# Keeping half instead of a quarter of one streamed weight chunk in SBUF, with a kept chunk's rest and the transposes moved in PSUM

## The chip, the cores and the metric

The kernel runs on one core of one Trainium2 chip. The metric is the device time of one execution in microseconds (us). Besides the matrix engine TensorE (PE, with its weight loads shown apart as PEld) the core has VectorE (DVE), ScalarE (ACT), GpSimd (POOL) and SyncE (SP). DMAs are issued from the queues of SP, ACT and POOL.

## The reference

Two independent results stand side by side in the output. Half A multiplies a shifted and weighted `k` by `v`, convolves it along 2048 positions with a long filter by way of FFTs, adds a skip term, and multiplies by `q`. Half B is a recurrent attention over 64 segments of 32 rows. Its loop is what matters here:

```python
mem = mem0                                        # 8 rows of 1024
for s in range(n_seg):                            # 64 segments
    h = concatenate([mem, x[:, 32*s:32*s+32]])    # 40 rows
    q = einsum('btd,dhe->bhte', h, Wq)            # 32 heads of 128; k and v alike
    p = softmax(where(mask, einsum('bhqe,bhke->bhqk', q, k) * scale, -1e9))
    o = einsum('bhqk,bhke->bhqe', p, v)
    o = einsum('bhte,hed->btd', o, Wo)
    mem = o[:, :8]                                # feeds the next segment
    outs.append(o[:, 8:])
```

The first eight rows of a segment's output are the memory of the next, so the segments run one after another. Wq, Wk, Wv and Wo are 1024 x 4096 (or 4096 x 1024) in bf16, 32 MB together, more than SBUF holds.

## The kernel before, in words

**Two stages.** The first 440 us or so compute half A (`a_kernel`), and beside it, by `fill` and `dense`, the queries, keys and values of the rows that every segment brings itself; these go to the DRAM tensors `REC` and `VBD`. `x_block` turns the rows of x, and stores them in `REC` with one DMA of GpSimd per four segments. In this stage a scheduler decides the order of instructions. The second stage is the loop over 64 segments; I call one turn of it a pass. Its order is written out by hand, under `tc.manual_schedule()`: each engine runs its instructions in the order of the code, and waits at each for what it needs.

**Weights.** A weight chunk is 128 x 2048 bf16, 512 KB. There are 64: eight each of (Wk, Wq, Wv) x two halves g, and sixteen of Wo. 48 live in SBUF for the whole loop (tiles `Wres`, `Wmid`, `Wmore`, `Wlate`, `pw`, `Wring`). The other 16 are streamed (`STREAM`). Two of those (`KEPT_A`, `KEPT_B`) are tucked away bit by bit in unused PSUM columns in pass 0 (`keep`), and in every later pass VectorE copies them back, a quarter at a time (`quarter`, `quarter_b`; in place of `wring`). So 14 come from the DRAM copy `WS` in every pass, through a ring of five slots `wring` (`fetch`, issued from SP in order: the next chunk goes out when PE has finished with the slot's old one). Of one of them, `PART`, which is the chunk of Wo for head pair 4, the first quarter of the columns stays in the SBUF tile `part`, and a pass streams the other 384 KB.

**A pass, in PE's order.** `Proj(m, g)` accumulates a projection in a PSUM bank: four 32-column matmuls for each of eight chunks, about 0.22 us for a chunk. K uses bank `acc0`, Q `acc1`, V the bank g. `evac` is ScalarE's copy of the result to SBUF (`qkv_sb`). Then `transposes` turns it on PE into PSUM, and VectorE (K and Q of g = 0) or ScalarE (g = 1) copies it out to `KT` or `QT`. The hand-written order puts other chunks between an evacuation and its transposes, to cover it. `scores`, `softmax_a`, `softmax_b`, `attend` follow for each g; `out_half` multiplies by Wo into `yacc` (the same two banks). `fill_mem` turns the eight memory rows of the result, through the PSUM tile `tps`, into the next pass's `hT` (`rec`).

**PSUM.** Each partition has eight banks of 2 KB: the banks `acc0` and `acc1`, one bank `tps` (two rows of 512 bf16), one bank `SB` for scores, four for `OTp`. Chunk `KEPT_B` has four quarters, spread over unused columns (`B_homes`); the last quarter is partly in SBUF (`B_rest`, 768 bytes), and PE reads that part straight from there. Before, the transposes of K0, Q0 and K1 go to `tps[:, 0, :]`, and those of Q1 to bank 1, whose name is then `turned`:

```python
q0.run(4)
KT0 = keys(0)
nc.vector.tensor_copy(KT0[:, :, :, 0:32], transposes(k0, True))
q0 = q0.run(2).evac()
...
nc.scalar.copy(KT1[:, :, :, 0:32], transposes(k1))
turned = transposes(q1, tp=bank(1, "turned")[:].bitcast(BF)[:, 0:512])
```

**Descriptors.** `set_scratch` cuts the room in which GpSimd's DMAs keep their descriptors to `SCRATCH` bytes in each partition.

Of the kernel before, what the change touches and what calls it, by code (L numbers as in the profile page):

```python
# [9 lines left out]
BF = mybir.dt.bfloat16  # L10
F32 = mybir.dt.float32
I32 = mybir.dt.int32
# [8 lines left out]

FIRST, LAST = (0, 1, 2, 3), (10, 15, 11, 12, 14)
KEPT_A, KEPT_B = (3, 13, 0), (3, 9, 0)
PART = (3, 4, 0)
O_ORDER = (*FIRST, 4, 5, 6, 7, 9, 13, 8, *LAST)
ORDER = [(0, kc, 0) for kc in (0, 1, 4, 5)] + [(1, kc, 0) for kc in (0, 1)] + [(0, kc, 0) for kc in (2, 3, 6, 7)] + \
    [(1, kc, 0) for kc in range(2, 8)] + [(m, kc, 1) for m in (0, 1) for kc in range(8)] + \
# [8 lines left out]
RING = 5  # L36

PITCH = 2048
SCRATCH = 1024


def set_scratch(nc, size):
    cut = nc.dynamic_dma_scratch_size - size
    nc.lookup_mloc("DynamicDMAScratchLoc").dims = [128, size]
    nc.lookup_mls("DynamicDMAScratchLoc").tensor_shape = [128, size]
    nc.dynamic_dma_scratch_size = size
    for name in ("const-float32-0.0", "const-float32-1.0", "const-bfloat16-1.0", "const-uint8-127"):
        loc = nc.lookup_mloc(name)
        loc.addr = loc.addr - cut
    nc.sbuf_base = nc.sbuf_base - cut  # L50
# [372 lines left out]
def b_kernel(ctx: ExitStack, tc, x, mem0, Wq, Wk, Wv, Wo, outb, n_seg, run_a):  # L423
    nc = tc.nc
# [27 lines left out]
    def dram_chunk(ch):  # L452
        m, a, g = ch
        return Wo_v[a] if m == 3 else W_v[m][a, g]

    def dst_view(ap, ch):
        return ap.rearrange("p (hh d) -> p hh d", hh=2) if ch[0] == 3 else ap

    def stream_src(ch):
        return WS[ring_order.index(ch), :, 0:2048]  # L460
# [3 lines left out]
    REC = dram.tile([128, n_seg, 768], BF, name="REC")  # L464
# [33 lines left out]
    def pw(k=None):  # L498
        if k is None:
            k = pw_next[0] % 8  # L500
            pw_next[0] += 1
        return pring.tile([128, 2048], BF, tag=f"pw{k}", name="pw")
# [89 lines left out]
    def x_block(b):  # L592
        X_sb = loaded.pop(b)
        if b % 2 == 0:
            t = base.tile([128, 2048], BF, tag="wring3", name="xt")
            xts[b], xts[b + 1] = t[:, 0:1024], t[:, 1024:2048]
        tp = ps0.tile([128, 1024], BF, tag="ps0", name="xt_ps")
        for kc in range(8):
            nc.tensor.transpose(tp[:, kc * 128:(kc + 1) * 128], X_sb[:, kc * 128:(kc + 1) * 128], ident[:])
        xt = xts.pop(b).rearrange("p (s k t) -> p s k t", s=4, k=8)  # L600
        rows = tp[:].rearrange("p (k j t) -> p j k t", k=8, j=4)
        nc.vector.tensor_copy(xt[:, :, :, NM:SEG], rows[:, :, :, 0:NX])
        nc.vector.tensor_copy(xt[:, :, :, 0:NM], rows[:, :, :, NX:SEG])
        rec_stores.append(nc.gpsimd.dma_start(REC[:, 4 * b:4 * b + 4, 0:256], xt.rearrange("p s k t -> p s (k t)")))

    xts = {}
    rec_stores, x_loads = [], []
# [39 lines left out]
    q1 = [None] * 8  # L647
# [46 lines left out]
    def more(i):  # L694
        return wres3.tile([128, 2048], BF, tag=f"Wmore{i}", name="Wmore")
# [10 lines left out]
    live = {}  # L706
    now = [0]
    free = [4, 5, 0, 1, 3]

    def slot():  # L710
        k = free.pop(0)
        t = (base if k < 4 else ring).tile([128, 2048], BF, tag=f"wring{k}", name="wring")
        return k, t

    def fetch():
        if loads:
            s, ch = loads.pop(0)
            live[s, ch] = k, t = slot()
            if ch in kept:
                nc.sync.dma_start(dst_view(t[:], ch), dram_chunk(ch))  # L720
            elif ch == PART:
                nc.sync.dma_start(t[:, 512:2048], stream_src(ch)[:, 512:2048])
            else:
                nc.sync.dma_start(t[:], stream_src(ch))

# [13 lines left out]
    with c0p:  # L739
# [5 lines left out]
        for i, ch in enumerate(v_temp):  # L745
            if i >= 2:
                home = (lambda i=i: more(i)) if i < len(v_temp) - 2 else (lambda k=i - len(v_temp) + 4: pw(k))
# [3 lines left out]
        with tc.issue_after(got[-1].ins):  # L751
            for _ in range(2):
                fetch()
        n_k = len(own[0, 0])
        late = late[n_k:-2] + late[4:n_k] + late[:4] + late[-2:]
        for g in range(2):
# [13 lines left out]
            if g == 0:  # L770
# [8 lines left out]
    one = ctx.enter_context(tc.tile_pool(name="b_one", bufs=1, side="right", reuse_waits="tile"))  # L779
# [7 lines left out]
    tps = ps_t.tile([128, 2, 512], BF, name="tps")  # L787
    SB = ps_s.tile([128, 512], F32, name="SB")
    S = SB[:, 0:320].rearrange("p (b k) -> p b k", b=8)
    OTi, tpi, SBi = OTp[:].bitcast(I32), tps[:].bitcast(I32), SB[:].bitcast(I32)  # L790
    B_rest = one.tile([128, 192], I32, name="B_rest")
    B_homes = [[(tpi[:, 1, :], 0)], [(SBi[:, 320:448], 0), (OTi[:, :, 480:512], 128)], [(OTi[:, :, 416:480], 0)],
               [(B_rest[:], 0), (SBi[:, 448:512], 192)]]

    def bits(dst, src):
        nc.vector.tensor_scalar(out=dst, in0=src, scalar1=0, scalar2=None, op0=ALU.bitwise_or)  # L796

    def like(ap, home):
        return ap.rearrange("p (b x) -> p b x", b=4) if len(home.shape) == 3 else ap

    def quarter_b(q, tag):
        t = one.tile([128, 256], I32, tag=tag, name="quarter_b")
        w = []
        for home, at in B_homes[q]:
            n = home.shape[1] * (home.shape[2] if len(home.shape) == 3 else 1)
            if home.shape == B_rest[:].shape:
                part = home.bitcast(BF)
            else:
                bits(like(t[:, at:at + n], home), home)
                part = t[:].bitcast(BF)[:, 2 * at:2 * at + 2 * n]  # L810
            for dh, o in enumerate(quarter_cols(q)):
                lo, hi = max(at, 128 * dh), min(at + n, 128 * dh + 128)
                if lo < hi:
                    w.append((o + 2 * lo - 256 * dh, o + 2 * hi - 256 * dh, part[:, 2 * (lo - at):2 * (hi - at)]))
        return w

    def quarter_cols(q):
        return [1024 * (q // 2) + 512 * dh + 256 * (q % 2) for dh in range(2)]
# [27 lines left out]
    def pieces(ch):  # L846
        if ch in res:
            return [(0, 2048, res[ch])]
        if now[0] == 0 and ch in at_hand:
            return [(0, 2048, at_hand[ch][0])]  # L850
        if ch == PART:
            return [(0, 512, part[:]), (512, 2048, live[now[0], ch][1][:, 512:2048])]
        return [(0, 2048, live[now[0], ch][1][:])]

    def columns(ps, a, b):
# [13 lines left out]
                place_late(1, lambda: base.tile([128, 2048], BF, tag="wring2", name="Wring"))  # L869
            fetch()  # L870

    part = one.tile([128, 512], BF, name="part")
    nc.sync.dma_start(part[:], dram_chunk(PART)[:, 0, 0:512])
    P_pad = one.tile([128, 5, 64], BF, name="P_pad")
    nc.vector.memset(P_pad[:], 0.0)

# [2 lines left out]
    def bank(k, name):  # L879
        return ps_acc.tile([128, 512], F32, tag=f"acc{k}", name=name)  # L880
# [6 lines left out]
    def turn_tile(dst, src):  # L887
        for e in range(0, 128, 32):
            nc.tensor.matmul(dst[e:e + 32, :], lhsT=src[:, e:e + 32], rhs=ident[:], start=True, stop=True,  # L889
                             is_transpose=True, tile_position=(0, e))  # L890
# [13 lines left out]
    with tc.manual_schedule():  # L904
        for _ in range(RING - 2):
            fetch()
# [15 lines left out]
        for s in range(n_seg):  # L922
# [7 lines left out]
            def keys(g):  # L930
                KT = one.tile([128, 4, 4, 40], BF, tag="KT", name="KT")
                nc.gpsimd.tensor_copy(KT[:, :, :, 32:40],  # L932
                                      KBs[:, 128 * g:128 * g + 128].rearrange("p (c i t) -> p i c t", c=4, i=4))
                return KT
# [22 lines left out]
                    nc.scalar.copy(sb[:], self.acc[:])  # L957
                    return sb

            def transposes(sb, tiles=False, tp=tps[:, 0, :]):  # L960
                for i in range(4):
                    dst, src = tp[:, i * 128:(i + 1) * 128], sb[:, i * 128:(i + 1) * 128]
                    if tiles:
                        turn_tile(dst, src)
                    else:
                        nc.tensor.transpose(dst, src, ident[:])  # L966
                return tp.rearrange("p (i c r) -> p i c r", i=4, c=4)
# [91 lines left out]
            k0 = Proj(0, 0).run(4)  # L1059
            q0 = Proj(1, 0)  # L1060
            fill_mem(hT, Y, 1)
            q0.run(2)
            k0 = k0.run(4).evac()
            q0.run(4)
            KT0 = keys(0)
            nc.vector.tensor_copy(KT0[:, :, :, 0:32], transposes(k0, True))  # L1066
            q0 = q0.run(2).evac()
            k1 = Proj(0, 1).run(4)
            QT0 = one.tile([128, 4, 4, 32], BF, tag="QT", name="QT")
            nc.vector.tensor_copy(QT0[:], transposes(q0, True))  # L1070
            k1 = k1.run(4).evac()
            scores(0, QT0, KT0)
            E0 = softmax_a()
            q1 = Proj(1, 1).run(4)
            KT1 = keys(1)
            PT0 = softmax_b(E0)
            q1 = q1.run(4).evac("QT")
            pv0 = Proj(2, 0).run(3)
            nc.scalar.copy(KT1[:, :, :, 0:32], transposes(k1))
            turned = transposes(q1, tp=bank(1, "turned")[:].bitcast(BF)[:, 0:512])  # L1080
            QT1 = one.tile([128, 4, 4, 32], BF, tag="rot", name="QT")
            nc.scalar.copy(QT1[:], turned)
            V0 = pv0.run(5).evac("QT")
# [51 lines left out]
def kernel(  # L1135
# [17 lines left out]
    assert int(B_seg_len) == 32  # L1153
    set_scratch(tc.nc, SCRATCH)
    S = B_x.shape[1]
# [47 lines left out]
```

## Time and profile before

| | |
|---|---|
| median of 3 runs | 1791.54 us (1789.31 to 1793.37) |
| the profiled execution | 1793.29 us, of which the instructions span 1791.4 us |
| PE busy, PEld busy | 1681.0 us, 994.8 us |
| DVE, ACT, POOL busy | 1038.7, 658.8, 301.2 us |
| moved by DMA | 623.31 MB, 348 GB/s on average |
| granted TensorE clock | 0.985 on average |
| streamed chunks | 831 of 512 KB and 64 of 384 KB |

The profile takes the times of one execution. PE's matmuls are pipelined and their ends are modelled, so busy shares of PE tell little; starts of successive groups tell more. "Idle before" of a group is the time that its engine stood still just before it, with what ended that. The chain of waits is followed back from the last instruction to whatever released each step.

### The profile page before, as it was taken

What the parts mean: (1) busy time and instruction counts of PE and PEld (TensorE: products, weight loads), DVE (VectorE), ACT (ScalarE), POOL (GpSimd) and SP (SyncE); (2) the same over time, 40 slices, a digit from 0 to 9 for tenths busy, and PEclk for the clock granted to TensorE, in tenths of its full rate; (3) what the DMA queues carried; (4) which work ended last, traced back from release to release, by engine and by line L of the source; (5) the groups of instructions that cost most, each with busy time, mean ns of one, the idle gap of its engine ahead of it and who ended that gap; (6) DMA issues with size and microseconds to landing.
All of it is one profiled execution on the core that took longest, in us unless ns stands there. A gap on an engine that the chain in (4) does not pass through costs nothing.

```text
span 1791.4 us, 70833 instructions
## 1 busy us (share of the span) xinstructions
PE 1681.0 (94%) x30776; PEld 994.8 (56%) x30776; DVE 1038.7 (58%) x3429; ACT 658.8 (37%) x1157; POOL 301.2 (17%) x563
## 2 busy tenths in 40 slices
PE   6989997798999999999999999999999999999998
PEld 2443333343566666656666666665666666666665
DVE  9926875433555555555555555565555555656555
ACT  6955650001333333333333333333333333333333
POOL 4002342100111111111111111111111111111111
PEclk9999998899999999999999999999999999999999
DMA  9989987998999999999999999999999999999998
GB/s 342 361 324 290 308 285 265 337 315 325 381 359 356 352 369 372 358 350 364 359 359 368 347 363 354 367 366 352 345 355 365 364 363 350 375 362 364 369 364 295
DMA packets 219756, 623.31 MB, mean 348 GB/s; under 512 B 57442, under 2 KB 57586, under 8 KB 219444
## 3 DMA queue, kind: packets, MB, share of 16 engines
q1 hardware_dynamic: 160948, 550.58, 83.6%
q0 software_dynamic: 19104, 45.13, 7.4%
q10 hardware_dynamic: 39392, 23.07, 4.3%
q8 instruction: 241, 3.95, 0.9%
q14 instruction: 71, 0.58, 0.1%
HBM read 563.63 MB, written 57.67 MB: 347 GB/s over the span
## 4 chain that ended last, share of the span: by engine, by line
PE 66%; DMA 19%; DVE 6%; ACT 4%; issue 3%; ACTq 1%; POOL 0%; SPq 0%; POOLq 0%; DVEq 0%
PE acc L948 30%; PE yacc L1038 19%; DMA wring<-WS 14%; PE kb_ps L624 5%; DMA REC<-stage 2%; ACT OT L1028 2%; PE tps L889 2%; ACT s_sb L249 1%; DVE E L983 1%; DVE mx L981 1%; PE tps L966 1%; PE s_ps L247 1%; ACTq L653 1%; PE turned L966 1%; PE vb_ps L765 1%
## 5 line engine op out<-in xcount | busy, mean ns | idle before, releaser
L1038 PEld LDWEIGHTS <-OT 128*64 128x64 bf16 x8255 | 438.8, 109 | 53.6 <-ACT OT L1028 35.6
L948 PEld LDWEIGHTS <-rec 128*32 128x32 bf16 x12288 | 293.7, 96 | 291.3 <-DVE rec L900 41.7
L957 ACT CAST qkv_sb<-acc 128x512 bf16<-128x512 f32 x384 | 224.7, 585 | 514.1 <-PE acc L948 353.0
L948 PE MATMUL acc<-Wres,rec 128*32 128x512 bf16 x3328 | 242.6, 380 | 2.6 <-issue 2.1
L948 PE MATMUL acc<-wring,rec 128*32 128x512 bf16 x2300 | 228.2, 382 | 17.2 <-DMA wring<-WS 14.0
L1038 PE MATMUL yacc<-Wmore,OT 128*64 128x256 bf16 (+1 forms) x2560 | 219.9, 274 | 0.0
L948 PE MATMUL acc<-Wmid,rec 128*32 128x512 bf16 x3072 | 211.3, 379 | 1.0 <-issue 1.0
L1038 PE MATMUL yacc<-wring,OT 128*64 128x256 bf16 x2448 | 194.9, 273 | 6.9 <-DMA wring<-WS 6.9
L1130 POOL DMA_DIRECT2D out_dram<-Y x128 | 64.6, 507 | 487.4 <-ACT Y L1128 484.4
L796 DVE TENSOR_SCALAR quarter<-OTp 128x256 int32<-128x256 int32 x252 | 99.9, 417 | 78.4 <-ACT OT L1028 78.4
L1128 ACT CAST Y<-yacc 128x256 bf16<-128x256 f32 x128 | 47.6, 372 | 256.8 <-DVE quarter_b L796 164.8
L1028 ACT CAST OT<-OTp 128x640 bf16<-128x640 f32 x128 | 87.4, 683 | 143.4 <-PE OTp L1020 143.4
L948 PE MATMUL acc<-pw,rec 128*32 128x512 bf16 x1796 | 132.7, 379 | 1.0 <-issue 1.0
L1066 DVE COPY KT<-tps 128x512 bf16<-128x512 bf16 x64 | 27.2, 425 | 155.0 <-PE tps L889 155.0
L900 DVE CAST rec<-tps 128x32 bf16<-128x32 f32 x128 | 24.5, 192 | 159.1 <-PE tps L898 155.7
L948 PE MATMUL acc<-Wlate,rec 128*32 128x512 bf16 x1536 | 116.4, 379 | 0.0
L884 POOL DMA_DIRECT2D rec<-REC x64 | 36.2, 565 | 448.4 <-PE acc L948 432.7
L981 DVE TENSOR_REDUCE mx<-SB 128x8 f32<-128x320 f32 x128 | 62.9, 492 | 67.1 <-PE SB L975 64.0
L986 ACT ACTIVATE E<-E 128x320 f32<-128x320 f32 x128 | 60.1, 470 | 82.0 <-DVE E L983 82.0
L624 PE MATMUL kb_ps<-XBT,pw 128*128 128x512 bf16 x320 | 82.9, 400 | 1.9 <-DMA pw<-in_B_Wk_dram 1.3
L1038 PE MATMUL yacc<-Wlate,OT 128*64 128x256 bf16 x1024 | 79.1, 276 | 5.4
L932 POOL COPY KT<-rec 128x128 bf16<-128x128 bf16 x128 | 38.8, 303 | 227.2 <-PE SB L975 220.6
(223 smaller groups left out, 2671.5 us busy)
## 6 DMA issues: line engine op xcount, KB each, us to landing
wring<-WS SPq DMA_DIRECT2D x831, 512.0 KB, 6.2
wring<-WS SPq DMA_DIRECT2D x64, 384.0 KB, 5.7
rec<-REC POOLq DMA_DIRECT2D x64, 192.0 KB, 5.7
SK<-s_sb SPq DMA_DIRECT2D x16, 512.0 KB, 4.5
SU<-s_sb SPq DMA_DIRECT2D x16, 512.0 KB, 5.7
Kg<-SK SPq DMA_DIRECT2D x32, 256.0 KB, 4.1
Ug<-SU SPq DMA_DIRECT2D x32, 256.0 KB, 5.5
REC<-stage ACTq DMA_DIRECT2D x16, 512.0 KB, 13.2
```

The costliest lines, as they stand in the source:

```text
L624: nc.tensor.matmul(ps[:], lhsT=ws[kc][:, hl * 128:(hl + 1) * 128], rhs=xbt(kc).rearrange("p s t -> p (s t)"), start=(kc == 0), stop=(kc == 7))
L796: nc.vector.tensor_scalar(out=dst, in0=src, scalar1=0, scalar2=None, op0=ALU.bitwise_or)
L884: nc.gpsimd.dma_start(rec[:], REC[:, s, :])
L932: nc.gpsimd.tensor_copy(KT[:, :, :, 32:40], KBs[:, 128 * g:128 * g + 128].rearrange("p (c i t) -> p i c t", c=4, i=4))
L948: nc.tensor.matmul(self.acc[32 * c:32 * c + 32, :], lhsT=hT[:, ch[1], :], rhs=w[:, 512 * c:512 * c + 512], start=(ch == chs[0]), stop=(ch ...
L957: nc.scalar.copy(sb[:], self.acc[:])
L981: nc.vector.tensor_reduce(out=mx[:], in_=S, op=ALU.max, axis=AX.X)
L986: nc.scalar.activation(E[:], E[:], ACT.Exp, scale=scale)
L1028: nc.scalar.copy(OT[:], o_view)
L1038: nc.tensor.matmul(yacc[f][64 * dh:64 * dh + m, x - o:y - o], lhsT=lhsT, rhs=r, start=(h == (0, 2 * FIRST[-1])[f] and x == o), stop=stop, ...
L1128: nc.scalar.copy(Y[:, 256 * f:256 * f + 256], yacc[f][:, 0:256])
L1130: nc.gpsimd.dma_start(bass.AP(outb.tensor, outb.offset + SEG * s * 2048 + 512 * dh, [[2048, 32], [1, 512]]), Y[64 * dh + NM:64 * dh + 40, :])
```

## The change

Three things are done together. First, `part` holds 1024 instead of 512 columns of the chunk `PART` (2 KB instead of 1 KB in each partition), so a pass streams 256 KB of it. Second, 768 + 512 bytes of SBUF in each partition become free: `B_rest` goes to PSUM, to the rest of the first row of `tps`, from where VectorE copies it to SBUF in every pass like the other homes; and `SCRATCH` is 512. `x_block` stores its rows (128 partitions by four segments) with two DMAs of half the size. Third, the row of `tps` is no longer free for transposes: those of K0 and Q0 go to the accumulator bank that their own evacuation has just emptied (K0 to bank 0, Q0 to bank 1), and those of K1 and Q1 to the two halves of bank 1. Of q0's last six chunks, three instead of four now stand ahead of K0's transposes, and three instead of two behind.

```diff
-PART = (3, 4, 0)
+PART, PART_COLS = (3, 4, 0), 1024
-SCRATCH = 1024
+SCRATCH = 512
...
-        rec_stores.append(nc.gpsimd.dma_start(REC[:, 4 * b:4 * b + 4, 0:256], xt.rearrange("p s k t -> p s (k t)")))
+        for h in (0, 2):
+            rec_stores.append(nc.gpsimd.dma_start(REC[:, 4 * b + h:4 * b + h + 2, 0:256],
+                                                  xt[:, h:h + 2].rearrange("p s k t -> p s (k t)")))
...
-                nc.sync.dma_start(t[:, 512:2048], stream_src(ch)[:, 512:2048])
+                nc.sync.dma_start(t[:, PART_COLS:2048], stream_src(ch)[:, PART_COLS:2048])
...
-    B_rest = one.tile([128, 192], I32, name="B_rest")
-               [(B_rest[:], 0), (SBi[:, 448:512], 192)]]
+               [(tpi[:, 0, 64:256], 0), (SBi[:, 448:512], 192)]]
...
-            if home.shape == B_rest[:].shape:
-                part = home.bitcast(BF)
-            else:
-                bits(like(t[:, at:at + n], home), home)
-                part = t[:].bitcast(BF)[:, 2 * at:2 * at + 2 * n]
+            bits(like(t[:, at:at + n], home), home)
+            part = t[:].bitcast(BF)[:, 2 * at:2 * at + 2 * n]
...
-            return [(0, 512, part[:]), (512, 2048, live[now[0], ch][1][:, 512:2048])]
+            return [(0, PART_COLS, part[:]), (PART_COLS, 2048, live[now[0], ch][1][:, PART_COLS:2048])]
...
-    part = one.tile([128, 512], BF, name="part")
-    nc.sync.dma_start(part[:], dram_chunk(PART)[:, 0, 0:512])
+    part = one.tile([128, PART_COLS], BF, name="part")
+    nc.sync.dma_start(part[:], dram_chunk(PART)[:, 0, 0:PART_COLS])
...
-            def transposes(sb, tiles=False, tp=tps[:, 0, :]):
+            def transposes(sb, bank_of, at=0, tiles=False):
+                tp = bank_of[:].bitcast(BF)[:, at:at + 512]
...
-            q0.run(4)
+            q0.run(3)
             KT0 = keys(0)
-            nc.vector.tensor_copy(KT0[:, :, :, 0:32], transposes(k0, True))
-            q0 = q0.run(2).evac()
+            nc.vector.tensor_copy(KT0[:, :, :, 0:32], transposes(k0, bank(0, "turned"), tiles=True))
+            q0 = q0.run(3).evac()
             k1 = Proj(0, 1).run(4)
             QT0 = one.tile([128, 4, 4, 32], BF, tag="QT", name="QT")
-            nc.vector.tensor_copy(QT0[:], transposes(q0, True))
+            nc.vector.tensor_copy(QT0[:], transposes(q0, bank(1, "turned"), tiles=True))
...
-            nc.scalar.copy(KT1[:, :, :, 0:32], transposes(k1))
-            turned = transposes(q1, tp=bank(1, "turned")[:].bitcast(BF)[:, 0:512])
+            turned = bank(1, "turned")
+            nc.scalar.copy(KT1[:, :, :, 0:32], transposes(k1, turned))
+            turned = transposes(q1, turned, 512)
```

## The prediction

> **What bounds the kernel now.** I read the summed busy times of a window first, to see what the loop of passes uses. From the first pass's end at 461 us to the last's at 1787.5 us:
>
> ```profile
> 461.00:1787.50 1326.50, 1290.15 (x28511) 829.41 (x28503) 754.94 (x2834) 475.29 (x882) 203.03 (x440) 1.00 0.98 360
> ```
>
> 63 passes in 1326.5 us are 21.06 us each. PE is busy for 1290 us, but the DMA engines for 0.98 of the time too, at 360 GB/s: two things run almost full, so the next question is what a pass takes when PE alone sets it. The chain of waits in order of time tells, by the same group of matmuls (the 44 ahead of K1's transposes) in successive passes:
>
> ```profile
> 1141.31 2.37 PE acc L948 x44
> ...
> 1163.15 2.37 PE acc L948 x44
> ...
> 1183.46 2.37 PE acc L948 x44
> ```
>
> 21.84 us, then 20.31. In the second interval the chain names no DMA; 20.31 also comes back between 1689.37 and 1709.68. So 20.31 us is what PE needs with every streamed chunk in time, and the mean pass holds 0.75 us of waiting above it. How much of that is the ring's? The groups by line, PE's alone:
>
> ```profile
> L948 PE MATMUL acc<-wring,rec 128*32 128x512 bf16 x2300 | 228.2, 382 | 17.2 <-DMA wring<-WS 14.0 <-DVE rec L900 1.2 <-issue 1.1
> ...
> L1038 PE MATMUL yacc<-wring,OT 128*64 128x256 bf16 x2448 | 194.9, 273 | 6.9 <-DMA wring<-WS 6.9
> ```
>
> The last columns are PE's idle time before streamed chunks: 17.2 + 6.9 = 24.1 us, or 0.38 us a pass, 20.9 us of it until a chunk landed (modelled ends hide some more). PE's order and the ring are thus nearly balanced, PE a little ahead. A stall added to PE in every pass counts almost in full, while a shorter stream can give back only these waits.
>
> Then I read the timeline around the transposes that move. K0's and Q0's, in one pass:
>
> ```profile
> 925.05 0.39 PE L948 MATMUL acc<-pw,rec 128*32 128x512 bf16 x4
> 925.27 0.82 PE L948 MATMUL acc<-Wmid,rec 128*32 128x512 bf16 x12
> 925.54 0.58 ACT L957 CAST qkv_sb<-acc 128x512 bf16<-128x512 f32 x1 [2.08 <-PE acc L948]
> 925.92 0.39 PE L948 MATMUL acc<-wring,rec 128*32 128x512 bf16 x4
> 926.18 0.41 PE L889 MATMUL tps<-ident,qkv_sb 128*32 128x128 bf16 x16
> 926.41 0.61 PE L948 MATMUL acc<-Wlate,rec 128*32 128x512 bf16 x8
> 926.63 0.42 DVE L1066 COPY KT<-tps 128x512 bf16<-128x512 bf16 x1 [2.29 <-PE tps L889]
> 926.84 0.82 PE L948 MATMUL acc<-Wmid,rec 128*32 128x512 bf16 x12
> 927.12 0.58 ACT L957 CAST qkv_sb<-acc 128x512 bf16<-128x512 f32 x1 [1.00 <-PE acc L948]
> 927.49 0.39 PE L948 MATMUL acc<-wring,rec 128*32 128x512 bf16 x4
> 927.76 0.41 PE L889 MATMUL tps<-ident,qkv_sb 128*32 128x128 bf16 x16
> ```
>
> K0's last chunk (`pw`) starts at 925.05; ScalarE evacuates from 925.54 to 926.12; four chunks of q0 cover it exactly, and K0's transposes start at 926.18. Then K1's and Q1's, a pass earlier:
>
> ```profile
> 910.16 0.82 PE L948 MATMUL acc<-Wres,rec 128*32 128x512 bf16 x12
> 910.39 0.58 ACT L957 CAST qkv_sb<-acc 128x512 bf16<-128x512 f32 x1 [0.18 <-PE acc L948]
> 910.91 0.40 PE L966 MATMUL tps<-ident,qkv_sb 128*128 128x128 bf16 x4
> 911.14 0.39 PE L966 MATMUL turned<-ident,qkv_sb 128*128 128x128 bf16 x4
> 911.40 0.58 ACT L1079 COPY KT<-tps 128x512 bf16<-128x512 bf16 x1 [0.43 <-PE tps L966]
> ```
>
> K1's start at 910.91, Q1's 0.23 us behind, while ScalarE copies K1's out of the other bank.
>
> **The change, part by part.** *The shorter stream.* 128 KB less at 360 GB/s is 0.36 us of DMA time a pass, 1.7% of the stream: 23 us over 63 passes if DMA alone set the pace. DMA needs 0.98 x 21.06 = 20.64 us a pass now, and some 20.3 then. The gain on PE is bounded by the 0.75 us of waiting, and by nothing from below.
>
> *K0's and Q0's transposes.* Three chunks ahead instead of four: PE is free at 925.92, but the evacuated K0 is there only at 926.18, as now. So PE stands for 0.26 us, and the chunk that covered it (0.22 us) follows later. Behind the transposes (0.23 us) stand three chunks, to 926.41 + 3 x 0.22 = 927.06. Then k1 starts in bank 0, from where VectorE now still copies K0 (926.63 to 927.05): it can start at about 927.11, against 926.84. Q0's evacuation starts 0.22 us later with its last chunk, ends at 927.92, and Q0's transposes start at 927.98 instead of 927.76: +0.22 us. Of the two delays, 0.05 us is slack that the second one uses. Bounds: nothing (in passes where PE waits for a chunk just there) and 0.27.
>
> *K1's transposes* go to bank 1, which holds q1 until ScalarE has evacuated it at 910.97; with the 0.06 us that such a release takes in these rows they start at 911.03: +0.12 us.
>
> *Q1's transposes* go to the same bank as K1's. In the changed program their first matmul carries a wait for ScalarE's copy of K1. That copy starts 0.49 us after K1's transposes (910.91 to 911.40) and takes 0.585; with 0.06 for the release, Q1's start 1.13 us behind K1's instead of 0.23: +0.90 us. PE works in order, so pv0's next chunk and all behind it wait. Nothing else can cover it. If disjoint columns of one bank were enough, as in the row where PE writes one bank while ScalarE reads another, the spacing would stay 0.23 and this term 0. [...]
>
> Together PE needs 20.31 + 0.22 + 0.12 + 0.90 = 21.55 us a pass. That is above DMA's 20.3, so the ring gets 1.2 us of slack in every pass. Of the 0.75 us of today's waiting I keep 0.25: the ring's 0.38 shrinks to about 0.1, and part of the rest (waits on "issue" and on ScalarE) stays. Bounds: 0 and 0.75. A pass then takes 21.80 us, +0.74; over 63 passes +46.6 us.
>
> *VectorE's new copy* of 192 words from `tps` costs some 0.33 us, between its 128-word (0.28) and 256-word (0.42) copies. VectorE is idle for 1.07 us behind the last `quarter_b` piece (921.39 to 921.62), and PE needs the piece at 922.27: ready at about 921.95, hidden by 0.3 us. Without that cover it would cost at most 0.33 a pass. ScalarE's copy of Q1 follows its transposes by 0.49 + 0.59 = 1.08 us, and the scores come 1.4 us behind them: hidden.
>
> *GpSimd.* 16 stores of 0.784 us become 32 of about 0.71 (the row of `WS` copies with 256 runs): 10 us more issue in the first stage, where POOL is busy for 57 of 145 us (140 to 285 us) and is 0% of the chain. Whether half the descriptor room makes it wait for earlier DMAs to drain, no row shows: at most until a landing, 6 us for each of the 16, and it would delay `Yre`, which waits 51.0 us for VectorE anyway. Two of Kg's and Ug's loads swap places on SP. I take +2 us for the first stage, between -3 and +12. In the loop POOL issues five DMAs a pass, and nothing moves. `part` loads 128 KB more, once: 0.4 us.
>
> Sum: 1791.4 + 46.6 + 2 = 1840 us of span. The profiled execution took 1793.3 us, 1.9 more than its span and 1.8 more than the median; against the median of 1791.5 the forecast is **1840 us**, +2.7%.
>
> **The rivals.**
>
> *DMA alone sets the pace (faster).* Then PE's new stalls hide under the stream, and 0.33 to 0.36 us a pass go: 1769 to 1771 us. For it speaks the DMA share of 0.98; against it, that passes of 20.31 us exist, and that DMA would have to need over 21.55 us where it now needs 20.64. Chance 0.04.
>
> *Q1's transposes don't wait for the copy* (no 0.90): PE needs 20.65, about what DMA needs; with 0.35 us of waiting the pass takes 21.0 us, and the whole 1788 to 1793 us. The program's wait speaks against it. 0.04.
>
> *The stalls are partly paid already.* Where PE waits for a chunk shortly before, K0's 0.22 vanishes, and with 0.1 of waiting left a pass takes 21.43: 1815 us. 0.17.
>
> *The waiting doesn't shrink.* If chunks come late at random, not for want of bandwidth, all 0.75 us stay: 22.3 a pass, 1870 us; with POOL held up in the first stage, 1881. 0.17.
>
> **How the numbers follow.** The forecast (1825 to 1855) gets 0.58. 1815 to 1865 holds 8 in 10: it leaves out the two rivals at or below the old time (0.08) and the outer half of the last two. About 0.2% can be told from no change here. Slower 0.92, within it 0.04, faster 0.04.
>
> **What would show it.** PE's idle time before the second group of `turned` matmuls of line 965 near 0.9 us a pass, put down to ScalarE's KT copy; K0's transposes at line 887 released by the evacuation, with 0.26 us of idle before them; an undisturbed pass of 21.5 instead of 20.3 us; waits for `wring` well under 24 us; DMA share about 0.94. I am wrong if passes of 20.3 us still occur, or if waits for the ring grow beside the new ones.

## The result and the profile after

The changed kernel takes 1908.78 us (median of four runs, 1901.22 to 1918.1); the kernel before took 1792.45 us beside it (1789.31 to 1797.52). The ratio is 1.065, with a 95% interval of 1.060 to 1.070. I had forecast 1840 us, and 1865 at most.

The profiled execution spans 1907.5 us, 116.1 more than before. I split it at the end of the first pass, which is the end of its second copy of Y. That point moved from 460.2 to 533.9 us: 73.7 us were lost ahead of it. The 63 passes behind it lost 42.3 us, from 1327.3 to 1369.6.

**The loop.** The summed busy times of the changed kernel, from the first pass's end to the last's (columns: window, its length, busy time and count of PE, PEld, DVE, ACT and POOL, granted clock, DMA share, GB/s):

```profile
533.90:1903.50 1369.60, 1299.40 (x28531) 841.18 (x28523) 770.05 (x2897) 481.57 (x883) 204.53 (x440) 1.00 0.95 343
```

A mean pass takes 1369.6 / 63 = 21.74 us. The DMA share fell from 0.98 to 0.95, at 343 instead of 360 GB/s. The chain of waits gives an undisturbed pass, and what is new in it:

```profile
1041.93 2.37 PE acc L946 x44
1044.34 0.40 PE turned L965 x4
1044.82 0.59 ACT KT L1079
1045.45 0.38 PE turned L965 x4
...
1063.43 2.37 PE acc L946 x44
```

21.50 us from one group of 44 to the next, where 20.31 were needed before. Between the two groups of transposes of line 965 now stands ScalarE's copy of K1: 1.11 us from start to start, where there were 0.23. The groups by line (last columns: idle time before them, and what ended most of it):

```profile
L946 PE MATMUL acc<-wring,rec 128*32 128x512 bf16 x2300 | 227.1, 382 | 10.4 <-DMA wring<-WS 8.8 <-DVE rec L898 1.4
...
L1037 PE MATMUL yacc<-wring,OT 128*64 128x256 bf16 x2320 | 187.4, 273 | 3.1 <-DMA wring<-WS 3.0
...
L965 PE MATMUL turned<-ident,qkv_sb 128*128 128x128 bf16 x512 | 49.1, 217 | 49.0 <-ACT KT L1079 46.6
```

The waits for streamed chunks went from 24.1 to 13.5 us, and 46.6 us of waiting for the KT copy came instead, some 0.73 us a pass.

**The first stage.** Here lies what I had missed. One piece of the timeline of POOL, before:

```profile
165.05 0.78 POOL L604 DMA_DIRECT2D REC<-xt  x1 [1.41 <-DVE xt L603]
165.83 0.55 POOL L679 DMA_DIRECT2D WS<-pw  x1
166.40 1.17 POOL L366 TENSOR_TENSOR Yre<-pa,pb 128x512 bf16<-128x512 bf16 x1
```

and the same place after:

```profile
164.48 0.72 POOL L605 DMA_DIRECT2D REC<-xt  x1 [1.30 <-DVE xt L603]
170.51 0.73 POOL L605 DMA_DIRECT2D REC<-xt  x1 [5.31 <-issue]
171.24 0.57 POOL L681 DMA_DIRECT2D WS<-pw  x1
171.82 1.16 POOL L366 TENSOR_TENSOR Yre<-pa,pb 128x512 bf16<-128x512 bf16 x1
```

The first half of the store lands 5.7 us after its issue, at 170.2. Only then does POOL issue the second half; for 5.31 us it stands, and the profile names no releaser ("issue"). `Yre`, which follows in POOL's order, starts 7.3 us behind the first store instead of 1.4. The waits of the stage (130 to 480 us) by engine, line and releaser, after (columns: us in total, times, longest):

```profile
POOL Yre L366 <- DVE pb L361: 105.5, 16, 56.6
ACT zs L379 <- PE z_ps L377: 72.7, 28, 11.8
POOL REC L605 <- issue: 67.7, 15, 8.7
PE z_ps L375 <- POOL Yre L366: 48.8, 12, 8.8
```

Before, the profile puts no wait of POOL's stores down to "issue", and two of these lines read:

```profile
POOL Yre L366 <- DVE pb L361: 51.0, 24, 6.4
...
ACT zs L379 <- PE z_ps L377: 23.4, 21, 3.5
```

Fifteen stores wait 67.7 us together, and the chain POOL, PE, ScalarE behind them waits with them. POOL's other DMAs of this stretch stand on "issue" too: 16.7 us before stores of half A's output (`out_dram`), 10.9 and 4.9 us before copies to `WS`, where 2.0 us stood before. Together that is about 100 us. The group of all `Yre` (count; shortest, median and longest duration in ns; first and last start) shows how much time that took, before and after:

```profile
L366 POOL TENSOR_TENSOR Yre<-pa,pb x34: 1141/1152/1392, 142.1 to 274.4; 128x512 bf16<-128x512 bf16 x32, 64x512 bf16<-64x512 bf16 x2
```

```profile
L366 POOL TENSOR_TENSOR Yre<-pa,pb x34: 1142/1155/1266, 141.6 to 338.9; 128x512 bf16<-128x512 bf16 x32, 64x512 bf16<-64x512 bf16 x2
```

The same 34 operations, each as long as before, are spread over 197.3 instead of 132.3 us. That is 65 of the 73.7 us.

The TensorE clock that was granted fell as well: from the start to the end of the first pass it was 0.88 on average instead of 0.94, and 0.77 instead of 0.86 between 230 and 340 us. With as many matmul records as before (2253), PE was busy for 411.6 instead of 390.1 us there. How much of these 21.5 us lies on the chain is not separated; they are part of the 73.7.

### The profile page after: what moved, and what is told of

It is laid out like the page before. It is cut to its first block, busy times and chain, and to the rows that moved or that the text cites. A ratio compares the mean times of both kernels' runs of the same rounds, so it can differ in the third digit from the quotient of the medians.

```text
span 1907.5 us, 70917 instructions
## 1 busy us (share of the span) xinstructions
PE 1711.0 (90%) x30776; PEld 1007.8 (53%) x30776; DVE 1051.8 (55%) x3492; ACT 665.9 (35%) x1157; POOL 313.3 (16%) x579
## 4 chain that ended last, share of the span: by engine, by line
PE 58%; DMA 11%; ACT 6%; issue 4%; DVE 4%; POOL 1%; SPq 0%; ACTq 0%; POOLq 0%; DVEq 0%
PE acc L946 25%; PE yacc L1037 21%; DMA wring<-WS 8%; PE vb_ps L767 3%; PE turned L965 3%; ACT OT L1027 2%; ACT KT L1079 2%; PE turned L887 2%; ACT qkv_sb L955 2%; DVE mx L980 2%; DVE E L982 2%; PE kb_ps L626 1%; DMA REC<-stage 1%; PE SB L974 1%; DMA zt<-SZ 1%
## 5 line engine op out<-in xcount | busy, mean ns | idle before, releaser
L946 PE MATMUL acc<-Wres,rec 128*32 128x512 bf16 x3328 | 236.4, 380 | 0.2 <-issue 0.2
L1037 PE MATMUL yacc<-wring,OT 128*64 128x256 bf16 x2320 | 187.4, 273 | 3.1 <-DMA wring<-WS 3.0
L946 PE MATMUL acc<-Wlate,rec 128*32 128x512 bf16 x1536 | 116.3, 379 | 0.0
L1065 DVE COPY KT<-turned 128x512 bf16<-128x512 bf16 x64 | 27.2, 425 | 153.8 <-PE turned L887 153.8
L965 PE MATMUL turned<-ident,qkv_sb 128*128 128x128 bf16 x512 | 49.1, 217 | 49.0 <-ACT KT L1079 46.6
```

Source lines behind the costliest of these rows:

```text
L946: nc.tensor.matmul(self.acc[32 * c:32 * c + 32, :], lhsT=hT[:, ch[1], :], rhs=w[:, 512 * c:512 * c + 512], start=(ch == chs[0]), stop=(ch ...
L1037: nc.tensor.matmul(yacc[f][64 * dh:64 * dh + m, x - o:y - o], lhsT=lhsT, rhs=r, start=(h == (0, 2 * FIRST[-1])[f] and x == o), stop=stop, ...
```

## The experiments

Two theories share the loss. *Room*: with half the descriptor room, POOL can't issue a DMA until an earlier one has landed, some 70 us in the first stage. *KT copy*: in the loop PE stands for ScalarE's copy out of the bank it wants to write, some 43 us. Rivals: the halved stores cost by themselves; the loop loses by its other edits; the shorter stream works for or against it. All medians below are set against runs of the kernel before on the same chip (1789.6 us for the first four, 1790.2 for the next four, 1790.8 for the last).

**1. Room and split alone**, on the kernel before:

```diff
-SCRATCH = 1024
+SCRATCH = 512
...
-        rec_stores.append(nc.gpsimd.dma_start(REC[:, 4 * b:4 * b + 4, 0:256], xt.rearrange("p s k t -> p s (k t)")))
+        for h in (0, 2):
+            rec_stores.append(nc.gpsimd.dma_start(REC[:, 4 * b + h:4 * b + h + 2, 0:256],
+                                                  xt[:, h:h + 2].rearrange("p s k t -> p s (k t)")))
```

> The kernel before with nothing but half the descriptor room (SCRATCH 512) and the split store. Theory 'room' (in the changed kernel the first pass ends 74 us later, because GpSimd stands in its DMA issues until earlier ones have landed, and Yre behind them): first pass ends near 534 us instead of 460, passes stay at 21.06 us, whole 1860 to 1870 us. Theory 'loop' (the first stage is late for another reason, for instance the other addresses and the other order of the scheduled stage, and half the room alone is hidden): first pass at 460 to 470 us, whole 1790 to 1802 us.

1860.12 us, ratio 1.039 (1.036 to 1.042). The first pass ends at 533.1 us, and a mean pass takes 21.02 us, as before. So these lines alone cost the first stage its 70 us, and nothing in the loop. The lower clock comes with them: up to the end of the first pass it is 0.88, with PE busy for 408.1 us, against 0.94 and 387.6 us in run 2 below, which has the same stores and the old room.

**2. The split alone**, with the room of 1024 (the second edit of the diff above without the first):

> The kernel before with the store of x_block split in two, and the full descriptor room. Theory 'room': the split costs some 10 us of GpSimd's issue, hidden; first pass at 458 to 464 us, whole 1789 to 1797 us. Theory 'split' (twice as many stores with twice as many landings are what delays the first stage): 1850 us or more.

1789.27 us, ratio 0.9995 (0.997 to 1.002). Two halves cost no more than one store. It is the room.

**3. The changed kernel with the old room**, one store again, and 768 instead of 1024 columns of `PART` kept, so that it fits into SBUF:

```diff
-PART, PART_COLS = (3, 4, 0), 1024
+PART, PART_COLS = (3, 4, 0), 768
...
-SCRATCH = 512
+SCRATCH = 1024
...
-        for h in (0, 2):
-            rec_stores.append(nc.gpsimd.dma_start(REC[:, 4 * b + h:4 * b + h + 2, 0:256],
-                                                  xt[:, h:h + 2].rearrange("p s k t -> p s (k t)")))
+        rec_stores.append(nc.gpsimd.dma_start(REC[:, 4 * b:4 * b + 4, 0:256], xt.rearrange("p s k t -> p s (k t)")))
```

> The changed kernel with the full descriptor room and one store again; to fit, part keeps 768 columns, so a pass streams 320 KB of it. Theory 'room' with the waits of the transposes: first pass at 460 us, an undisturbed pass 21.5, the mean 21.75 us, whole 1832 to 1840 us. If the transposes' waits were not what lengthens the pass: 1785 to 1800 us. If the first stage is late without the half room: 1900 us.

1840.66 us, ratio 1.029 (1.026 to 1.032). The first pass ends at 464.9 us, a mean pass takes 21.75. The transposes wait for the KT copy for 46.6 us, as in the changed kernel. The losses of runs 1 and 3, 70.5 and 51.1 us, add up to 121.6; the whole change lost 116.3.

**4. The shorter stream alone**: the kernel before with 256 KB of `PART` in the stream, as in the changed kernel. A quarter of that chunk's columns is left out of the product.

```diff
-                nc.sync.dma_start(t[:, 512:2048], stream_src(ch)[:, 512:2048])
+                nc.sync.dma_start(t[:, 1024:2048], stream_src(ch)[:, 1024:2048])
...
-            return [(0, 512, part[:]), (512, 2048, live[now[0], ch][1][:, 512:2048])]
+            return [(0, 512, part[:]), (512, 1024, part[:]), (1024, 2048, live[now[0], ch][1][:, 1024:2048])]
```

> The kernel before, streaming 256 instead of 384 KB of the chunk PART, and nothing else; columns 512 to 1023 of that chunk are replaced by columns 0 to 511 of it, so that part of the product is left out. My step (the gain is bounded by the 0.75 us of waiting in a pass; an undisturbed pass stays at 20.31): mean pass 20.75 to 20.9 us, whole 1772 to 1782 us. Theory 'DMA alone sets the pace': 20.7 us, 1768 to 1771 us. Theory 'chunks come late at random': no change, 1788 to 1795 us.

1789.03 us, ratio 1.0007 (0.999 to 1.003), a mean pass of 21.02 us, the undisturbed one 20.31. My expectation of 1772 to 1782 us missed. Runs 1, 2 and 8, whose loop is that of the kernel before, have mean passes of 20.96 to 21.08 us, so 21.02 is no gain. The DMA engines moved 354 instead of 360 GB/s and were still busy for 0.97 of the loop. So the saving that the change was to pay for with its other edits is not there, even without them.

**5. K1's transposes early**, from run 3:

```diff
+            nc.scalar.copy(KT1[:, :, :, 0:32], transposes(k1, bank(0, "turned")))
             PT0 = softmax_b(E0)
             q1 = q1.run(4).evac("QT")
-            pv0 = Proj(2, 0).run(3)
-            turned = bank(1, "turned")
-            nc.scalar.copy(KT1[:, :, :, 0:32], transposes(k1, turned))
-            turned = transposes(q1, turned, 512)
+            pv0 = Proj(2, 0).run(4)
+            turned = transposes(q1, bank(1, "turned"))
...
-            V0 = pv0.run(5).evac("QT")
+            V0 = pv0.run(4).evac("QT")
```

> The changed kernel with the old descriptor room and the single store (and 768 instead of 1024 columns kept, so that it fits), as in the run before with these, which took 1840.7 us; and K1's transposes go, behind four chunks of q1, into bank 0, which K1's own evacuation has emptied, so that Q1's stand alone in bank 1 behind four chunks of pv0 and wait for no copy of KT. If the wait for ScalarE's KT copy is what the loop lost: PE's 0.73 us of idle time a pass goes, an undisturbed pass falls from 21.46 to 20.5-20.65 us (20.31 + 0.22 for K0 and Q0, + up to 0.1), the mean to 20.95-21.25 as the chunks' waits return, and the whole to 1788-1808 us. If the loop lost it elsewhere (K0's and Q0's stalls, VectorE's new copy), the pass stays above 21.3 us and the whole above 1825 us.

1807.16 us, ratio 1.009 (1.007 to 1.012). The wait is gone, and of run 3's 51.1 us of loss 17.0 are left. The undisturbed pass is 20.82 to 20.88 us, not 20.5 to 20.65, and the mean 21.27. The mean and the whole lie at the upper end of what I had expected. What is left above 20.65 lies at the transposes, which now stand in two places: a group of four takes 0.33 us to the next group, and the chunks ahead of each take 0.10 to 0.12 us more than other chunks, each time that PE goes over from 32-column to 128-column work.

**6. Three quarters of the room**: the changed kernel with `SCRATCH` 768 and one store. From here on I count a DMA by its runs, that is, the pieces of it that are contiguous in memory by the program's shapes: a whole store of x's rows has 512, a half 256, a copy of a weight chunk 128 or 256.

> The changed kernel with 768 instead of 512 bytes of descriptor room in each partition, and the store of x's rows as one DMA again. The stall in the first stage was 70 us with 512 bytes and none with 1024. [...] If any cut below 1024 makes each store wait for the one before, the first pass ends near 533 us and the whole takes 1900-1915 us.

1854.96 us, ratio 1.035 (1.032 to 1.039); the first pass ends at 480.0 us, the loop is that of the changed kernel (21.75 us). Most of the stall is gone; the case of 533 us does not hold. What is left is in POOL's timeline:

```profile
284.66 0.82 POOL L604 DMA_DIRECT2D REC<-xt  x1 [1.36 <-DVE xt L603]
291.11 0.67 POOL L673 DMA_DIRECT2D WS<-in_B_Wo_dram  x1 [5.63 <-issue]
291.70 1.25 POOL L366 TENSOR_TENSOR Yre<-pa,pb 64x512 bf16<-64x512 bf16 x1
```

A whole store (512 runs) goes out without a wait on "issue" here, but a copy of 256 runs behind it stands for 5.63 us.

**7. The store from ScalarE's queue**, with 512 bytes of room and 1024 columns, and with K1's transposes early as in run 5:

```diff
-        for h in (0, 2):
-            rec_stores.append(nc.gpsimd.dma_start(REC[:, 4 * b + h:4 * b + h + 2, 0:256],
-                                                  xt[:, h:h + 2].rearrange("p s k t -> p s (k t)")))
+        rec_stores.append(nc.scalar.dma_start(REC[:, 4 * b:4 * b + 4, 0:256], xt.rearrange("p s k t -> p s (k t)")))
```

> The changed kernel, with its 512 bytes of descriptor room and its 1024 kept columns, with two edits: the store of x's rows is issued from ScalarE's queue, as one DMA, and K1's transposes go early into bank 0. If the two losses are GpSimd's standing before its stores (+70 us) and the wait for the KT copy (+45 us), and nothing else, both go: first pass at 462-475 us, mean pass 20.95-21.2 us, the whole 1782-1808 us. If ScalarE, which now issues 16 stores in the first stage, holds up the evacuations there, the first pass ends after 480 us. If GpSimd's other DMAs (the copies of the weights) stall for want of room by themselves, the first pass stays above 500 us and the whole above 1825 us.

1832.23 us, ratio 1.022 (1.018 to 1.026). The loop is that of run 5 (mean pass 21.28 us; the 64 KB less of stream made no difference). The first pass ends at 488.3 us, 26.8 us later than in run 5. POOL still waits on "issue" before three stores of half A's output, 18.2 us, and most issues on ScalarE took 0.38 us, but one 6.66. The scheduler also put the stage in another order. Of the 26.8 us, 22.8 are lost already at the first `Yre` (162.9 us, against 140.1 in run 5), before ScalarE issues its first store at 178.9 us; so ScalarE's issues are not the main cost. In that stretch five copies of Wo's chunks (`WS<-in_B_Wo_dram`) now go out between 42 and 78 us, the first of which leaves at 242 us in run 5, and between 25 and 90 us POOL stands on "issue" for 40.5 us, against 15.9 in run 5. So the small room costs time here too; how much of the 22.8 us it costs stays open. By its number the first pass falls under my second case (after 480 us), but not by the cause that I gave there.

**8. Four stores of 128 runs**, on the kernel before with 512 bytes of room:

```diff
-        rec_stores.append(nc.gpsimd.dma_start(REC[:, 4 * b:4 * b + 4, 0:256], xt.rearrange("p s k t -> p s (k t)")))
+        for h in range(4):
+            rec_stores.append(nc.gpsimd.dma_start(REC[:, 4 * b + h:4 * b + h + 1, 0:256],
+                                                  xt[:, h:h + 1].rearrange("p s k t -> p s (k t)")))
```

> The kernel before, with 512 bytes of descriptor room and each store of x's rows cut into four of 128 runs. With two of 256 runs the second one waited for the first to land (about 5 us), and the whole took 1860 us. [...] If every DMA of GpSimd behind a store waits for the store's landing, there are three waits of 4-6 us a block and the whole takes over 1900 us. If smaller DMAs always fit, the whole is 1790-1800 us.

1830.01 us, ratio 1.021 (1.018 to 1.025); the first pass ends at 499.4 us. Neither of the two cases holds. POOL's timeline:

```profile
163.04 1.64 POOL L605 DMA_DIRECT2D REC<-xt  x3 [1.30 <-DVE xt L603]
168.67 0.54 POOL L605 DMA_DIRECT2D REC<-xt  x1 [3.99 <-DVE pd L363]
```

Three stores go out back to back. The fourth goes when the first has landed (163.04 + 5.3). The releaser printed, VectorE's `pd`, does not fit: the store starts 0.3 us behind that landing, as the second halves do in run 1. With twice as many DMAs as in run 1, the stall is little more than half.

**9. The pair first**, from run 3: PE turns K1 and Q1 into the two halves of bank 1, and only then ScalarE copies.

```diff
-            nc.scalar.copy(KT1[:, :, :, 0:32], transposes(k1, turned))
+            turned_k = transposes(k1, turned)
             turned = transposes(q1, turned, 512)
+            nc.scalar.copy(KT1[:, :, :, 0:32], turned_k)
```

> The changed kernel with the old descriptor room, the single store and 768 kept columns (1840.7 us, undisturbed pass 21.46), with one line moved: PE turns K1 and Q1 into the two halves of bank 1 right behind each other, and only then ScalarE copies the two. If the loss is the wait of Q1's transposes for ScalarE's copy out of the same bank, 0.8-0.9 us of PE time a pass goes: undisturbed pass 20.6-20.75 us (20.31 + 0.22 + 0.12), mean 21.0-21.2, the whole 1790-1805 us. If the later copies (KT's starts 0.23 us later) are late for the scores, PE stands before SB<-KT,QT instead and the undisturbed pass stays above 20.9 us. If two rows of transposes in one bank cost by themselves, the pass stays above 21.3 us.

1806.56 us, ratio 1.009 (1.007 to 1.012). One moved line, and of run 3's 51.1 us of loss 15.8 are left. The idle time before the transposes of line 963 falls from 49.0 to 2.5 us over the whole run. But the undisturbed pass is 20.81 us, a little above my 20.6 to 20.75, the mean 21.32 (21.0 to 21.2), and the whole 2 us above its range. The timeline of such a pass, PE first, then ScalarE:

```profile
600.05 0.61 PE L963 MATMUL turned<-ident,qkv_sb 128*128 128x128 bf16 x8
...
601.88 0.28 PE L969 MATMUL SB<-KT,QT 128*32 128x40 bf16 x16
```

```profile
600.75 0.59 ACT L1079 COPY KT<-turned 128x512 bf16<-128x512 bf16 x1 [0.75 <-PE turned L963]
601.24 0.59 ACT L1081 COPY QT<-turned 128x512 bf16<-128x512 bf16 x1
```

ScalarE's second copy ends at 601.83, and the scores start at 601.88: they now follow the copy directly. Both theories were partly right: the wait for the KT copy was the loss, and some 0.2 us of it comes back because the copies end later.

**10. K0 and Q0 alone**, on the kernel before:

```diff
-            q0.run(4)
+            q0.run(3)
             KT0 = keys(0)
-            nc.vector.tensor_copy(KT0[:, :, :, 0:32], transposes(k0, True))
-            q0 = q0.run(2).evac()
+            nc.vector.tensor_copy(KT0[:, :, :, 0:32], transposes(k0, True, tp=bank(0, "turned")[:].bitcast(BF)[:, 0:512]))
+            q0 = q0.run(3).evac()
...
-            nc.vector.tensor_copy(QT0[:], transposes(q0, True))
+            nc.vector.tensor_copy(QT0[:], transposes(q0, True, tp=bank(1, "turned")[:].bitcast(BF)[:, 0:512]))
```

> The kernel before with one part of the change: K0's and Q0's transposes go to the bank that their own evacuation has emptied, and three instead of four of q0's chunks stand ahead of K0's. By the prediction's step PE loses 0.22 us a pass: undisturbed pass 20.53 us. If the chunks' waits shrink with it, the mean stays at 21.05-21.15 us and the whole takes 1790-1797 us; if the waits are independent of PE's pace, the mean is 21.25-21.3 us and the whole 1802-1807 us.

1799.07 us, ratio 1.0035 (1.001 to 1.006). The undisturbed pass is 20.53 us, to the hundredth what I had worked out; the mean rises only from 21.06 to 21.12. The median is 2 us above the range that I gave for that mean, within what the first stage scatters (the first pass ends between 459.9 and 464.9 us in the kernels with the old room).

**11. K1 and Q1 alone**, on the kernel before:

```diff
-            nc.scalar.copy(KT1[:, :, :, 0:32], transposes(k1))
-            turned = transposes(q1, tp=bank(1, "turned")[:].bitcast(BF)[:, 0:512])
+            turned = bank(1, "turned")[:].bitcast(BF)
+            nc.scalar.copy(KT1[:, :, :, 0:32], transposes(k1, tp=turned[:, 0:512]))
+            turned = transposes(q1, tp=turned[:, 512:1024])
```

> The kernel before with another part of the change: K1's and Q1's transposes go to the two halves of bank 1, ScalarE copying K1's out in between. By the prediction's steps PE loses 0.12 + 0.90 us a pass: undisturbed pass 21.33 us, 0.7-0.9 us of idle time a pass before the second group of transposes, put down to the KT copy; mean 21.5-21.7 us, the whole 1820-1832 us. If the wait costs little because PE would have stood for chunks anyway, the whole is below 1812 us.

1831.25 us, ratio 1.024 (1.021 to 1.027). Undisturbed pass 21.29 us (+0.98 against the 1.02 of the prediction), mean 21.63. This is the loop's loss, and the two parts together (20.31 + 0.22 + 0.98 = 21.51) make the pass of the changed kernel.

**12. One chunk less**, on the kernel before: `PART` isn't streamed, and three quarters of its columns are left out of the product.

```diff
-             if s == 0 and ch not in v_temp[2:] or s > 0 and ch not in kept]
+             if ch != PART and (s == 0 and ch not in v_temp[2:] or s > 0 and ch not in kept)]
...
-            return [(0, 512, part[:]), (512, 2048, live[now[0], ch][1][:, 512:2048])]
+            return [(o, o + 512, part[:]) for o in range(0, 2048, 512)]
...
-        elif ch in streamed and (now[0] == 0 or ch not in kept):
+        elif ch != PART and ch in streamed and (now[0] == 0 or ch not in kept):
```

> The kernel before with the chunk PART not streamed at all: 13 instead of 14 chunks go through the ring in a pass, 384 KB or 5.4 % less. The resident quarter stands in for the other three quarters of the columns, so that part of the product with Wo is left out of the computation. A cut of 128 KB of the same chunk gained nothing (1789 us). If a pass is held up for want of bandwidth, a cut of 384 KB frees it: mean pass 20.35-20.6 us, the whole 1745-1762 us. If what holds it up is when a slot of the ring comes free and how long a chunk then takes to land, one chunk fewer for five slots frees it as well, 1745-1765 us, and the waits for the ring nearly vanish. If 0.7 us of waiting per pass has nothing to do with the stream, the whole stays at 1780-1792 us.

1766.94 us, ratio 0.987 (0.985 to 0.989), 5 and 2 us above the two ranges I had given. The undisturbed pass stays at 20.31 us, the mean falls to 20.62, and the groups that take streamed chunks hardly wait:

```profile
L948 PE MATMUL acc<-wring,rec 128*32 128x512 bf16 x2300 | 228.0, 382 | 3.7 <-DMA wring<-WS 1.8 <-DVE rec L900 1.2 <-issue 0.5
...
L1038 PE MATMUL yacc<-wring,OT 128*64 128x256 bf16 x2064 | 156.7, 273 | 0.9 <-DMA wring<-WS 0.9
```

So the stream does hold up PE, by some 0.44 us a pass, but 128 KB less of it gave nothing (run 4; nor did 64 KB in the pairs of runs 3 and 6, 5 and 7, whose mean passes agree within 0.02 us), where a third of 0.44 us over 63 passes would have been 9 us. Whether the bytes or the turn of a ring slot made the difference, these runs leave open.

## Why the prediction was wrong

**The step that failed is GpSimd's term**: "+2 us for the first stage, between -3 and +12". Measured were 73.7 us in the trace and 70.5 in run 1. The prediction had named the event and its size, "at most until a landing, 6 us for each of the 16", which is 96 us; then it set that against `Yre`, "which waits 51.0 us for VectorE anyway", and kept 12 as its bound. That cover did not exist. In the changed kernel `Yre` waits for VectorE for 105.5 - 56.6 = 48.9 us (the 56.6 is the one long wait ahead of the first `Yre`; before it is put down to a DMA, 58.2 us, and isn't in the 51.0). It is as much as before, and POOL's 67.7 us of waiting came on top. PE waits for `Yre` (48.8 us, 2.7 before), ScalarE for PE (72.7 instead of 23.4). When a stalled engine's partners wait for it in turn, its own wait for them is no slack to be used up. The second error was to look at POOL's share of the chain, 0%, as if it said what a stall there would cost.

The prediction also said that "no row shows" whether POOL waits for earlier DMAs. One did, in POOL's timeline before:

```profile
273.02 0.81 POOL L604 DMA_DIRECT2D REC<-xt  x1 [1.36 <-DVE xt L603]
273.82 0.70 POOL L673 DMA_DIRECT2D WS<-in_B_Wo_dram  x1
...
279.63 0.81 POOL L604 DMA_DIRECT2D REC<-xt  x1 [3.92 <-DVE stage L615]
```

The store issued at 273.02 lands 6.3 us later, and the next one goes 0.31 us behind that landing. Its rows `xt` had been ready since 277.90, and the store at 273.02 went 0.45 us behind its own. In the changed kernel 19 of the 32 stores start 0.30 to 0.34 us behind the landing of an earlier DMA of POOL (the fifteen above, and four whose wait is printed with another releaser), so the releaser printed here says little. The eight kernels with 1024 bytes and one store for each block all have this late store, 1.6 to 1.9 us behind its `xt` and 0.31 us behind the landing. By these rows the room was full for a moment even before the change.

The count that fits all of it could thus have been made beforehand, in the runs of a DMA as the program's shapes give them. Two more pieces of POOL's timeline before:

```profile
252.44 0.79 POOL L604 DMA_DIRECT2D REC<-xt  x1 [0.49 <-DVE xt L603]
253.23 0.71 POOL L673 DMA_DIRECT2D WS<-in_B_Wo_dram  x1
...
257.14 1.36 POOL L673 DMA_DIRECT2D WS<-in_B_Wo_dram  x2 [1.99 <-issue]
```

```profile
323.57 0.54 POOL L580 DMA_DIRECT2D WS<-pw  x1 [0.91 <-DMA pw<-in_B_Wq_dram]
324.10 0.72 POOL L418 DMA_DIRECT2D out_dram<-ot  x1
329.44 0.80 POOL L604 DMA_DIRECT2D REC<-xt  x1 [4.61 <-DVE xt L603]
```

Behind a store and a copy (512 + 256) the next copy of 256 runs stands for 1.99 us, and goes 0.31 us behind the landing of the store. The store at 329.44 is released by its own rows, while a copy of 128 runs and a store of 256 are under way: 896 runs with its own. So 1024 bytes held 896 runs at a time, but not 1024. An estimate from these rows, if the room goes by its bytes: half of it holds 448 runs, but not 512, the two halves of one store. The other runs agree: a room of 512 bytes held 384 at a time (256 + 128 in the changed kernel, three times 128 in run 8), but not 512 (256 + 256, 5.31 us of waiting at 170.51; the fourth 128 of run 8, 3.99 us); 768 bytes held 512, but not 512 + 256 (run 6, 5.63 us). The most that POOL's DMAs had under way at one time was 384 runs in the four kernels with 512 bytes, 640 with 768, and 896 in the nine with 1024. In what form the room holds a DMA no run shows; that POOL stands in its order until a landing is told by the traces.

**The loop's terms were right.** K0's and Q0's 0.22 us: 0.22 in run 10. K1's and Q1's 0.12 + 0.90: 0.98 in run 11. Undisturbed pass 21.55: 21.50. Of the 0.75 us of waiting I kept 0.25: 21.74 - 21.50 = 0.24. So 42.3 us of the +46.6 forecast came. The 0.24 was right in sum and not in its parts: the waits at streamed chunks kept 13.5 us, 0.21 a pass, not 0.1, and the rest nearly vanished; that the two errors cancel was luck. The 0.90 rested on the wait for the KT copy that the program carries, and the trace shows PE stand there for 0.73 us a pass; no run here shows what would happen without the wait.

How much of PE's loss the waiting takes back is a finding of its own: the undisturbed pass and the mean above it are 20.31 and 0.75 (before), 20.53 and 0.60 (run 10), 20.81 and 0.51 (run 9), 20.87 and 0.40 (run 5), 21.29 and 0.34 (run 11), 21.50 and 0.24 (the changed kernel). In these six kernels some 0.4 us of the waiting went for each us that PE became slower. "The waiting doesn't shrink" (1870 us) is thereby out for the loop, as is "the stalls are partly paid already": undisturbed passes of 21.50 us are the rule. "DMA alone sets the pace" and "Q1's transposes don't wait" are out as well.

**The signs.** The wait before the second group of line 965 is there (0.73 instead of 0.9 us; modelled ends hide the rest), the DMA share is 0.95 (0.94), the waits for `wring` are 13.5 us. Of the 0.26 us of idle time before K0's transposes the profile shows only some 0.09 a pass (5.5 us over 64), though the spacing moved by the full 0.22. Nothing in my list of signs looked at the first stage, and the last rival's "POOL held up" was priced at 11 us from the same wrong bound.

**The shorter stream** was bounded by 0.75 us a pass and gave nothing. Beside the KT copy's wait at most the 0.24 us that are left could have gone; run 4 shows that it is worth nothing without that wait either.

No version here that moves the transposes beats the kernel before: runs 5 and 9 are at 1.009 of its time, run 10, which moves only K0's and Q0's, at 1.0035.

## What to carry to other kernels

Before you cut the descriptor room of an engine's DMAs (here from 1024 to 512 bytes, 70.5 us in run 1), count what the DMAs under way at one time take of it (up to 896 runs here), and treat an issue that doesn't fit as a wait of that engine until a landing, with everything behind it in its order late by as much. Idle time of an engine covers such a wait only if what ends that idle time does not itself hang on the engine. Where two results of PE share a PSUM bank, let PE write both before another engine reads the first: that order alone was worth some 35 us here (runs 3 and 9).

## What the runs showed of the hardware that I had not expected

- In the changed kernel POOL's issues of the stores stood for 1.8 to 8.7 us until an earlier DMA of POOL had landed: the profile puts it down to "issue", or to whatever else came last, as to `pd` in run 8. The median from issue to landing of the changed kernel's 32 stores is 4.4 us, and the mean of the fifteen waits 4.5 us, so a wait was about one landing.
- A saving of 128 KB a pass (1.8% of the stream) at a DMA share of 0.98 was worth nothing (run 4: 0.999 to 1.003), while 384 KB with its whole chunk was worth 1.3% (run 12). A share near 1 did not mean that each byte counts: with fewer bytes the rate fell from 360 to 354 GB/s, at a share of 0.97.
- Two groups of four 128-column transposes took some 0.2 us more when they stood apart (run 5: twice 0.33 us, and 0.10 to 0.12 us ahead of each) than side by side (before: 0.55 us, and 0.10 ahead). Run 5's whole pass is 0.29 to 0.35 us above 20.31 + 0.22; the rest of that is not traced.
